# Instruction order, gate per four heads and the late weights of an attention and expert kernel

## The chip, the cores and the metric

The kernel runs on one core of one Trainium2 chip. The metric is the device time of one launch in microseconds (us), so less is better. The profile is one execution of the program, recorded by the hardware profiler.

## The reference

Windowed attention with a few global tokens is followed by a mixture of experts in which each expert keeps its 80 best tokens. There are 8 batches, 8 heads, 512 local and 32 global tokens of 64 values a head. A local query sees the local keys within 32 positions and all global keys; a global query sees every key. The 4352 token rows of 512 values then go through a gate of 8 experts.

```python
s_ll = np.where(np.abs(pos[:, None] - pos[None, :]) <= 32, scale * q_l @ k_l.T, -1e9)
a_l = sm(np.concatenate([scale * q_l @ k_g.T, s_ll], axis=-1))
out_l = a_l @ np.concatenate([v_g, v_l])
out_g = sm(scale * q_g @ np.concatenate([k_g, k_l]).T) @ np.concatenate([v_g, v_l])
x = np.concatenate([out_g, out_l], axis=2).transpose(0, 2, 1, 3).reshape(4352, 512)
logits = x @ w_gate                      # 512 x 8
expert = argmax(logits); gate_w = softmax(logits)[expert]
for e in range(8):                       # w1: 512 x 1024, w2: 1024 x 512
    tok = the 80 tokens of expert e with the largest gate_w
    out[tok] = gate_w[tok] * (relu(x[tok] @ w1[e]) @ w2[e])
```

All other rows of the output are zero.

## The kernel before

**Attention** runs in 16 steps, q = 0 to 15: a step is four heads of one batch (batch b = q // 2, quad qd = q % 2). Within a step the work is laid out by hand, and each engine runs its instructions in the order in which the program lists them. Step q computes the scores of step q + 1 and the outputs of step q:

- `load_qk` (L125) loads queries and keys as fp16 on POOL's queue, three steps ahead; `load_v` (L136) loads v on SP's queue, a batch ahead; `spread_v` (L145) copies v to `v_odd`, shifted by half a block, on POOL, and `spread_vg` (L210) the global v of four heads into the block-diagonal `vgbd`.
- `transpose_qk` (L234) transposes queries and keys on VectorE (DVE). `setup_globals` (L226) transposes the global queries and keys and spreads them into `qbd` and `kbd`, which must be cleared before.
- `S_heads` (L249) makes the local scores of two heads on TensorE (PE) and their exponentials on ScalarE (ACT). `S_globals` (L273) makes the scores with the global keys (L278), those of the global queries (L284), and the global-global ones (L279), which go into a free corner of the output tile of the running step.
- `O_pair` (L293) multiplies by v for half of the tokens, `norm` (L313) divides by the sums on DVE, `O_global` (L324) and `norm_global` (L336) do the same for the global queries.
- `x_rows` (L347) transposes the rows for the gate (L355), converts them to bf16 (ACT) and writes them to a DRAM scratch (SP). Once per batch `gate_logits` (L393), `gate_turn` (L410) and `gate_rest` (L420) compute the gate: `a0` to `a2` on DVE with one exponential, `a3` transposes the scores on PE into a list (`tp`, L462), `a4` packs row numbers and gate weights on POOL.
- `top_steps` (L486) finds the 80 best of a list in ten rounds of 8 on DVE. Three groups of batches have a list each; four rounds are done per step while there are any.

PSUM tiles come from two tags of two buffers each: S (`l_ps`, `lg`, `g_ps`, `lp`, `tp`) and O (`o_ps`). The bf16 weights of experts 0 and 1 are loaded in pieces of 256 KB during the steps (`load_w_piece`, L160).

**After attention** its pools are closed (`astack.close()`, L588), and the weights of experts 2 to 7 are issued on POOL (L593 to 596), then small constants, the clearing of `xg`, and the clearing of the rest of `pa` (L618). DVE does the last top-k, a tournament between the 64 list rows (L628, L629) that reads `pa`, the threshold and the positions; TensorE turns them into row numbers `idx`. POOL gathers the rows of the eight experts (L686), and each expert runs `F_turn` (L691), the hidden layer (L709 to 711), the output layer (L717) and the scaling by DVE into `y` (L719), a tile of three buffers:

```python
y = rpool.tile([cap, DF], FP32, tag="y", bufs=3, name=f"y{e}")
```

which POOL scatters to the output (L720). Rows that no expert takes get zeros, written by SP during the steps (`zeros`, L173).

## Time and profile before

| | us |
|---|---|
| median of 3 runs | 402.11 (400.72 to 407.21) |
| the profiled execution | 402.52 |
| its span, first to last instruction | 400.7 |
| TensorE busy | 219.0 (55%) |
| VectorE busy | 186.7 (47%) |
| POOL busy | 145.4 (36%) |
| ScalarE busy | 88.0 (22%) |

The profiled execution lies within the runs, so its rows can be used for the median. Busy shares are means over stages of different kinds; they have to be read stage by stage. L numbers are lines of the kernel before. PE is TensorE's matmuls, PEld its weight loads. The clock is the share of full speed that was granted to TensorE: 1.00 is 2.4 GHz, 0.50 is 1.2 GHz.

### The profile page before, as it was taken

The page shows a single profiled execution, that of the slowest core. Times are in us where ns is not written, and L with a number is a line of the kernel's source. Part 1 is how long each engine was busy: PE and PEld are TensorE (multiplying, and loading weights), DVE is VectorE, ACT ScalarE, POOL GpSimd, SP SyncE. Part 2 cuts the span into 40 slices and gives each one's busy share as a digit, 9 for nine tenths or more (in the row PEclk, how much of TensorE's full clock was granted, in tenths as well). Part 3 has the DMA queues.
Part 4 walks back from the last instruction along what each step waited for, and adds up shares of the span by engine and source line. Part 5 has one row for each costly group of instructions (what it writes and reads, how often), then busy time and mean ns, then how long its engine had stood idle before and what let it go on. Part 6 is the DMA issues. An engine that isn't in the chain of part 4 may idle for free. (4 is left out here: it accounts for less than half of the span.)

```text
span 400.7 us, 9267 instructions
## 1 busy us (share of the span) xinstructions
PE 219.0 (55%) x3944; PEld 154.4 (39%) x3944; DVE 186.7 (47%) x457; ACT 88.0 (22%) x153; POOL 145.4 (36%) x306
## 2 busy tenths in 40 slices
PE   1508729857857958859759759722000000347882
PEld 0306516635636736536536536511000000244561
DVE  5435665535554549667536538676700001811221
ACT  1202313325314224234324234220000000001220
POOL 8164512065074064047055053024444444052121
PEclk9966977979978786888977977955555555556999
DMA  8989247709809709907908803212999999011111
GB/s 151 177 152 240 49 79 149 201 0 181 246 16 188 224 0 181 246 2 139 277 12 159 269 0 69 97 76 70 198 209 210 209 209 207 5 41 43 34 50 33
DMA packets 60713, 51.10 MB, mean 128 GB/s; under 512 B 43904, under 2 KB 44672, under 8 KB 60672
## 3 DMA queue, kind: packets, MB, share of 16 engines
q0 software_dynamic: 19456, 27.79, 38.9%
q1 hardware_dynamic: 40112, 22.45, 21.3%
q8 instruction: 31, 0.51, 0.5%
q10 hardware_dynamic: 1104, 0.27, 0.3%
q14 instruction: 10, 0.08, 0.1%
HBM read 61.63 MB, written 14.68 MB: 190 GB/s over the span
## 5 line engine op out<-in xcount | busy, mean ns | idle before, releaser
L269 ACT ACTIVATE eL<-l_ps 128x1024 f32<-128x1024 f32 x32 | 32.8, 1024 | 98.4 <-PE l_ps L265 98.4
L473 POOL TENSOR_TENSOR rv<-oh,tb 128x160 bf16<-128x160 f32 x8 | 3.6, 456 | 136.5 <-DVE den L451 127.5
L303 PE MATMUL o_ps<-v_nat,eL 128*64 128x65 f32 x512 | 43.7, 248 | 1.3 <-issue 1.2
L303 PE MATMUL o_ps<-v_odd,eL 128*64 128x65 f32 x512 | 43.7, 249 | 0.0
L303 PEld LDWEIGHTS o_ps<-v_nat,eL 128*64 128x64 f32 x512 | 38.9, 160 | 5.2 <-issue 3.2
L308 PE MATMUL o_ps<-vgbd,eG 128*128 128x260 f32 x128 | 39.9, 437 | 0.0
L303 PEld LDWEIGHTS o_ps<-v_odd,eL 128*64 128x64 f32 x512 | 38.9, 160 | 0.0
L265 PE MATMUL l_ps<-qT,kT 32*64 32x128 f16 (+1 forms) x1152 | 26.8, 243 | 20.3 <-DVE kT L243 20.3
L642 PE MATMUL thr_ps<-dthr,ones 8*128 8x8 f32 x2 | 0.6, 352 | 66.0 <-DVE dthr L640 66.0
L265 PEld LDWEIGHTS <-kT 32*64 32x64 f16 x1152 | 20.3, 125 | 40.1 <-DVE kT L243 22.5
L711 ACT ACTIVATE fhT<-h_ps 128x320 bf16<-128x320 f32 x16 | 7.0, 437 | 111.5 <-DMA xgr<-x_scr,idx 83.7
L342 DVE RECIPROCAL rg<-o_ps 128x1 f32<-128x1 f32 x16 | 2.7, 169 | 56.4 <-PE o_ps L333 56.4
L253 PE MATMUL l_ps<-band,ident 128*128 128x512 f16 x64 | 25.4, 488 | 3.9 <-DMA band<-cband 3.9
L288 ACT ACTIVATE eG<-g_ps 128x1024 f32<-128x1024 f32 x16 | 16.4, 1024 | 46.2 <-PE g_ps L284 46.2
L642 PEld LDWEIGHTS thr_ps<-dthr,ones 8*128 8x128 f32 x2 | 0.5, 308 | 66.1 <-issue 66.1
L308 PEld LDWEIGHTS o_ps<-vgbd,eG 128*128 128x128 f32 x128 | 23.8, 207 | 4.9
L213 POOL COPY vgbd<-vg 32x65 f32<-32x65 f32 x64 | 15.2, 237 | 28.7 <-PE o_ps L333 18.7
L330 PE MATMUL o_ps<-v_nat,eG 128*32 128x65 f32 x512 | 14.5, 275 | 20.1 <-ACT egg L290 18.9
L628 DVE TENSOR_TENSOR pb<-pa 64x64 f32<-64x64 f32 x4 | 0.9, 218 | 49.7 <-POOL pa L618 49.6
L162 POOL DMA_DIRECT2D w1sb<-in_moe_w_dram x32 | 17.3, 541 | 17.0 <-DMA w1sb<-in_moe_w_dram 13.8
L320 DVE TENSOR_TENSOR xn<-o_ps,rec 128x512 f32<-128x512 f32 x32 | 22.1, 692 | 1.1
L165 POOL DMA_DIRECT2D w2sb<-in_moe_w_dram x32 | 17.2, 542 | 12.4 <-DMA w2sb<-in_moe_w_dram 12.3
(134 smaller groups left out, 479.5 us busy)
## 6 DMA issues: line engine op xcount, KB each, us to landing
out_dram<-zt SPq DMA_DIRECT2D x17, 512.0 KB, 7.2
w1sb<-in_moe_w_dram POOLq DMA_DIRECT2D x32, 256.0 KB, 9.7
w2sb<-in_moe_w_dram POOLq DMA_DIRECT2D x32, 256.0 KB, 7.1
v_nat<-in_v_l_dram SPq DMA_DIRECT2D x56, 128.0 KB, 5.7
raw<-in_q_l_dram POOLq DMA_DIRECT2D x16, 256.0 KB, 5.1
raw<-in_k_l_dram POOLq DMA_DIRECT2D x16, 256.0 KB, 7.6
x_scr<-xb SPq DMA_DIRECT2D x8, 512.0 KB, 6.5
v_nat<-in_v_l_dram SPq DMA_DIRECT2D x16, 64.0 KB, 6.3
```

Of the source, the lines that this page charges most:

```text
L162: nc.gpsimd.dma_start(out=w1sb[e][:, k], in_=moe_w1[e, 128 * k:128 * k + 128])
L165: nc.gpsimd.dma_start(out=w2sb[e][:, k].rearrange("p r f -> p (r f)"), in_=moe_w2[e, 256 * k:256 * k + 256].rearrange("(p r) f -> p (r f)" ...
L213: nc.gpsimd.tensor_copy(out=vgbd[q % 2][r, h], in_=vg[r, q])
L253: nc.tensor.matmul(out=l_ps[:, k], lhsT=ident16[:], rhs=band[:], start=True, stop=False, skip_group_check=True)
L265: nc.tensor.matmul(out=l_ps[o:o + 64, k, 64 * lo:64 * hi], lhsT=kv[r, m], rhs=qv[r, lo:hi], start=False, stop=(c2 == 1), tile_position=(32 ...
L269: nc.scalar.activation(out=eL[:], in_=l_ps[:], func=AF.Exp, scale=scale)
L288: nc.scalar.activation(out=eG[:], in_=g_ps[:], func=AF.Exp, scale=scale)
L303: nc.tensor.matmul(out=o[64 * odd:64 * odd + 64, k, 65 * h:65 * h + 65], lhsT=s["eL"][h][:, 64 * t:64 * t + 64], rhs=v[:, 4 * qd + h, u, : ...
L308: nc.tensor.matmul(out=o[:, k, 0:260], lhsT=s["eG"][:, 0, 128 * u:128 * u + 128], rhs=vgbd[q % 2][:].rearrange("p h d -> p (h d)"), start= ...
L320: nc.vector.tensor_tensor(out=s["xn"][:, 2 * j:2 * j + 2].rearrange("p u (h x) -> p u h x", x=64), in0=ov[:, :, :, 0:64], in1=rec[:].unsqu ...
L330: nc.tensor.matmul(out=og[32 * h:32 * h + 32], lhsT=s["eG"][:, 1, 128 * u + 32 * h:128 * u + 32 * h + 32], rhs=v[:, 4 * qd + h, u, :], sta ...
L711: nc.scalar.activation(out=hT[:, 4 * half:4 * half + 4, :], in_=hv, func=AF.Relu, scale=1.0)
```

## The change

The program before the steps, the order within a step, and what follows attention are laid out anew.

- **Before the steps:** `vg` is loaded in two parts, the first two quads ahead of v. Most clearing of `vg`, `vgbd`, `kbd` and `qbd` moves to DVE, for `kbd` and `qbd` only the first two quads; POOL clears the rest later. The scores of step 0 come ahead of `setup_globals`; q = 1 is transposed there too; `load_g(slice(2, 16))` moves behind the first spreads, `setup_gate` and the spread of the second half of v to the end of step 0. Constants of the routing are loaded and cleared in step 1.
- **Within a step:** `O_global` and the new `S_gg` (the global-global scores) come directly after the second `O_pair`, ahead of its norm. `x_turn` holds the transposes for the gate. `gate_logits` now does four heads at a time, those of step q - 2; `gate_turn` adds both halves. `first` holds a0 to a2; a3 and a4 come a step later, and the top-k rounds with them: three per step, five in the last two.
- **After attention:** pools are split so that the gate's tiles (`gate`, left side) outlive attention's (right side). The late weights get a pool at the right side. Two loads of 1 MB bf16 an expert take the place of eight pieces: three experts' ahead of the last `a4` and the clearing, three behind the gathers. A partition of w1 now holds four neighbouring rows instead of rows 128 apart, and `F_turn` reads the tokens with a stride to match; the pieces of w1 cover 32 partitions each.

```diff
-    astack = ExitStack()
-    apool = astack.enter_context(tc.tile_pool(name="attn", bufs=1))
-    lpool = astack.enter_context(tc.tile_pool(name="loads", bufs=2))
-    hpool = astack.enter_context(tc.tile_pool(name="heads", bufs=2))
+    gstack, astack = ExitStack(), ExitStack()
+    gpool = gstack.enter_context(tc.tile_pool(name="gate", bufs=2))
+    apool = astack.enter_context(tc.tile_pool(name="attn", bufs=1, side="right"))
+    hpool = astack.enter_context(tc.tile_pool(name="heads", bufs=2, side="right"))
...
+    def load_w1(e):
+        nc.gpsimd.dma_start(out=w1sb[e][:].rearrange("p c f -> p (c f)"),
+                            in_=moe_w1[e].rearrange("(p c) f -> p (c f)", c=4))
+
+    def load_w2(e):
+        nc.gpsimd.dma_start(out=w2sb[e][:].rearrange("p c r f -> p c (r f)"),
+                            in_=moe_w2[e].rearrange("(c p r) f -> p c (r f)", p=P, r=2))
+
     def load_w_piece(e, k):
         if k < 4:
-            nc.gpsimd.dma_start(out=w1sb[e][:, k], in_=moe_w1[e, 128 * k:128 * k + 128])
+            r = slice(32 * k, 32 * k + 32)
+            nc.gpsimd.dma_start(out=w1sb[e][r].rearrange("p c f -> p (c f)"),
+                                in_=moe_w1[e].rearrange("(p c) f -> p (c f)", c=4)[r])
...
     load_g(slice(0, 2))
     load_qk(1)
-
     ident16 = cpool.tile([P, P], FP16, name="ident16")
     nc.scalar.dma_start(out=ident16, in_=cd["ident16"].ap())
     band = apool.tile([P, 512], FP16, name="band")
     nc.scalar.dma_start(out=band, in_=cd["band"].ap().rearrange("p t i -> p (t i)"))
-
-    for i in range(2):
-        nc.vector.memset(v_nat[i][:, :, :, 64:65], 1.0)
+    identf = cpool.tile([P, P], FP32, name="identf")
+    nc.scalar.dma_start(out=identf, in_=cd["identf"].ap())
+    wgl = cpool.tile([32, 16, E], FP32, name="wgl")
+    nc.scalar.dma_start(out=wgl, in_=moe_w_gate.rearrange("(c f) e -> f c e", f=32))
+    rmask5 = cpool.tile([P, NSLOT * E], FP32, name="rmask5")
+    nc.scalar.dma_start(out=rmask5, in_=cd["rmask5"].ap().rearrange("p s e -> p (s e)"))
+    rmask = cpool.tile([P, E, NT], FP32, name="rmask")
+    nc.scalar.dma_start(out=rmask, in_=cd["rmask"].ap())
+
     kbd = apool.tile([P, NQ, 2, P], FP16, name="kbd")
     qbd = apool.tile([P, NQ, 2, P], FP16, name="qbd")
     vg = apool.tile([P, NQ, 65], FP32, name="vg")
     vgbd = [apool.tile([P, 4, 65], FP32, name=f"vgbd{i}") for i in range(2)]
     for i in range(2):
-        nc.gpsimd.memset(vgbd[i][:], 0.0)
-    nc.gpsimd.memset(vg[:, :, 64:65], 1.0)
-    nc.vector.memset(kbd[:], 0.0)
-    nc.vector.memset(qbd[:], 0.0)
+        nc.vector.memset(v_nat[i][:, :, :, 64:65], 1.0)
+    for bd in (kbd, qbd):
+        nc.vector.memset(bd[:, 0:2], 0.0)
+    nc.vector.memset(vg[:, :, 64:65], 1.0)
+    for i in range(2):
+        nc.vector.memset(vgbd[i][:], 0.0)
+    nc.sync.dma_start(out=vg[:, 0:2, 0:64], in_=v_g[0].rearrange("(q h) g d -> (h g) q d", h=4))
     load_v(0, slice(0, 4))
-    nc.sync.dma_start(out=vg[:, :, 0:64], in_=v_g.rearrange("b (q h) g d -> (h g) (b q) d", h=4))
+    nc.sync.dma_start(out=vg[:, 2:NQ, 0:64],
+                      in_=v_g.rearrange("b (q h) g d -> (h g) (b q) d", h=4)[:, 2:NQ])
+    load_v(0, slice(4, 8))
...
+    def S_gg(q, gg_ps):
+        for c2 in range(2):
+            nc.tensor.matmul(out=gg_ps, lhsT=kbd[:, q, c2], rhs=gT[:, 0, q, c2], start=False,
+                             stop=(c2 == 1), skip_group_check=True)
+
     def S_globals(q, gg_ps):
         s = st[q]
         g_ps = psS(f"g_ps{q}")
         for c2 in range(2):
             qv = qT[q][:, c2, :, 4:36].rearrange("x i (t r) -> x t i r", r=4)
             nc.tensor.matmul(out=g_ps[:, 0], lhsT=kbd[:, q, c2], rhs=qv, start=(c2 == 0), stop=(c2 == 1))
-            nc.tensor.matmul(out=gg_ps, lhsT=kbd[:, q, c2], rhs=gT[:, 0, q, c2], start=False,
-                             stop=(c2 == 1), skip_group_check=True)
...
+    def x_turn(q):
+        b, qd = divmod(q, 2)
+        bs = bst[b]
+        xT = gpool.tile([P, 8, 4, 32], FP32, tag="xT", name=f"xT{q}")
+        nc.vector.transpose(out=xT[:].rearrange("x c u i -> x u c i"),
+                            in_=st[q]["xn"][:].rearrange("p u (c x) -> p u c x", c=8))
+        xgT = gpool.tile([P, 2, 32], FP32, tag="xgT", name=f"xgT{q}")
+        nc.vector.transpose(out=xgT[:].rearrange("x c g -> x (c g)"), in_=bs["xg"][:, qd])
+        bs["xT", qd] = xT, xgT
...
+    def gate_logits(q):
+        b, qd = divmod(q, 2)
         bs = bst[b]
-        lg = psS(f"lg{b}")
-        for cc in range(16):
-            k = cc % 4
-            nc.tensor.matmul(out=lg[32 * k:32 * k + 32, 0, 0:128], lhsT=wgbd[:, cc],
-                             rhs=bs["xT"][cc // 8][:, cc % 8].rearrange("x u i -> x (u i)"),
-                             start=(cc < 4), stop=(cc >= 12), tile_position=(0, 32 * k), skip_group_check=True)
+        xT, xgT = bs["xT", qd]
+        lg = psS(f"lg{q}")
+        for j in range(8):
+            k = j % 4
+            nc.tensor.matmul(out=lg[32 * k:32 * k + 32, 0, 0:128], lhsT=wgbd[:, 8 * qd + j],
+                             rhs=xT[:, j].rearrange("x u i -> x (u i)"),
+                             start=(j < 4), stop=(j >= 4), tile_position=(0, 32 * k), skip_group_check=True)
+        for c2 in range(2):
+            nc.tensor.matmul(out=lg[0:8, 1, 0:32], lhsT=wgg[:, qd, c2], rhs=xgT[:, c2],
+                             start=(c2 == 0), stop=(c2 == 1), skip_group_check=True)
+        if qd == 0:
+            bs["lgs"] = gpool.tile([P, 2, 160], FP32, tag="lgs", name=f"lgs{b}")
+        nc.scalar.copy(out=bs["lgs"][:, qd, 0:128], in_=lg[:, 0, 0:128])
+        nc.scalar.copy(out=bs["lgs"][0:8, qd, 128:160], in_=lg[0:8, 1, 0:32])
...
+        for qd in range(2):
+            nc.tensor.transpose(out=lp[0:32, 1, 8 * qd:8 * qd + 8], in_=lgs[0:8, qd, 128:160],
+                                identity=identf[0:8, 0:8])
...
-        return [a0, a1, a2, a3, a4]
+        def first():
+            a0()
+            a1()
+            a2()
+
+        return [first, a3, a4]
...
-    setup_globals(slice(0, 2))
     transpose_qk(0, 0)
     transpose_qk(0, 1)
-    load_g(slice(2, 16))
+    S_heads(0, (0, 1))
+    S_heads(0, (2, 3))
+    setup_globals(slice(0, 2))
+    transpose_qk(1, 0)
+    transpose_qk(1, 1)
     load_qk(2)
-    nc.gpsimd.dma_start(out=tb, in_=cd["tb"].ap())
     spread_v(0, 0, 0)
     spread_v(0, 0, 1)
     spread_vg(0)
-    nc.gpsimd.memset(zt, 0.0)
-    setup_gate()
-    nc.gpsimd.memset(sc_all[:], 0.0)
-    for g in range(len(GROUPS)):
-        nc.gpsimd.memset(gp[g][:], 0.0)
-    for i in range(2):
-        nc.gpsimd.memset(Lt[i][:, 4, :], 0.0)
-    spread_v(0, 1, 0)
-    spread_v(0, 1, 1)
-    S_heads(0, (0, 1))
-    S_heads(0, (2, 3))
+    load_g(slice(2, 16))
+    for bd in (kbd, qbd):
+        nc.gpsimd.memset(bd[:, 2:], 0.0)
     gg0 = psO("gg0")
     nc.tensor.matmul(out=gg0[:, 1, 0:128], lhsT=ident16[:], rhs=ident16[:], start=True, stop=True)
+    S_gg(0, gg0[:, 1, 336:368])
     S_globals(0, gg0[:, 1, 336:368])
-    transpose_qk(1, 0)
-    transpose_qk(1, 1)
+    nc.gpsimd.memset(zt, 0.0)
 
     topq = []
-    pend = {}
+    gq = {}
     for q in range(NQ):
         b, qd = divmod(q, 2)
         nxt = q + 1 < NQ
@@ -535,6 +560,16 @@
         if qd == 0 and b + 1 < B:
             load_v(b + 1, slice(0, 8))
         zeros(1)
+        if q == 1:
+            for t, n in ((tb, "tb"), (tri, "tri"), (identbf, "identf"), (iota1, "iota1")):
+                nc.gpsimd.dma_start(out=t, in_=cd[n].ap())
+            nc.gpsimd.memset(sc_all[:], 0.0)
+            for g in range(len(GROUPS)):
+                nc.gpsimd.memset(gp[g][:], 0.0)
+            for i in range(2):
+                nc.gpsimd.memset(Lt[i][:, 4, :], 0.0)
+            nc.gpsimd.memset(onesb, 1.0)
+            nc.gpsimd.memset(ones8, 1.0)
 
         if nxt:
             S_heads(q + 1, (0, 1))
@@ -542,70 +577,78 @@
         if q + 2 < NQ:
             transpose_qk(q + 2, 0)
         norm(q, 0, o0)
-        if qd == 1 and b >= 1:
-            gate_logits(b - 1)
+        if q >= 2:
+            gate_logits(q - 2)
         if nxt:
             S_heads(q + 1, (2, 3))
         o1 = O_pair(q, 1)
+        O_global(q, o1[:, 1, 264:329])
+        if nxt:
+            S_gg(q + 1, o1[:, 1, 336:368])
         if q + 2 < NQ:
             transpose_qk(q + 2, 1)
         if q >= 1:
+            x_turn(q - 1)
+        norm(q, 1, o1)
+        norm_global(q, o1[:, 1, 264:329])
+        if nxt:
+            S_globals(q + 1, o1[:, 1, 336:368])
+        if q >= 1:
             x_rows(q - 1)
+        if qd == 0 and b >= 2:
+            gq[b - 2][1]()
         if qd == 1 and b >= 1:
             gate_turn(b - 1)
-            steps = gate_rest(b - 1)
-            for f in steps:
-                f()
+            gq[b - 1] = gate_rest(b - 1)
+            gq[b - 1][0]()
             bst.pop(b - 1)
-            for g, m in enumerate(GROUPS):
-                if m[-1] == b - 1:
-                    topq += top_steps(lst[g][:], lst[g + 1][:, 0:cap])
-        norm(q, 1, o1)
-        if nxt:
-            S_globals(q + 1, o1[:, 1, 336:368])
-        O_global(q, o1[:, 1, 264:329])
-        norm_global(q, o1[:, 1, 264:329])
+        if q == 0:
+            setup_globals(slice(2, 16))
+            setup_gate()
+            spread_v(0, 1, 0)
+            spread_v(0, 1, 1)
         if nxt:
             spread_vg(q + 1)
-        if q == 0:
-            setup_globals(slice(2, 16))
         if qd == 1 and b + 1 < B:
-            spread_v(b + 1, 0, 0)
-            spread_v(b + 1, 0, 1)
-            spread_v(b + 1, 1, 0)
-            spread_v(b + 1, 1, 1)
-        for _ in range(4):
+            for j in range(2):
+                spread_v(b + 1, j, 0)
+                spread_v(b + 1, j, 1)
+        if qd == 0 and b >= 2:
+            gq[b - 2][2]()
+            for g, m in enumerate(GROUPS):
+                if m[-1] == b - 2:
+                    topq += top_steps(lst[g][:], lst[g + 1][:, 0:cap])
+        for _ in range(5 if q >= 14 else 3):
             if topq:
                 topq.pop(0)()
+    x_turn(NQ - 1)
+    gate_logits(NQ - 2)
+    gate_logits(NQ - 1)
+    x_rows(NQ - 1)
     for f in topq:
         f()
-    x_rows(NQ - 1)
-    gate_logits(B - 1)
     gate_turn(B - 1)
-    for f in gate_rest(B - 1):
-        f()
+    gq[B - 1] = gate_rest(B - 1)
+    gq[B - 2][1]()
+    gq[B - 1][0]()
+    gq[B - 1][1]()
     zeros(17)
     astack.close()
+    wlate = ctx.enter_context(tc.tile_pool(name="wlate", bufs=1, side="right"))
+
+    def load_late(e):
+        alloc_w(e, wlate, bufs=E - NRES)
+        load_w1(e)
+        load_w2(e)
+
+    for e in range(NRES, 5):
+        load_late(e)
+    gq[B - 2][2]()
+    gq[B - 1][2]()
+    gstack.close()
...
-    w2pool = ctx.enter_context(tc.tile_pool(name="wlate", bufs=1))
-    for e in range(NRES, E):
-        alloc_w(e, w2pool, bufs=E - NRES)
-        for k in range(8):
-            load_w_piece(e, k)
-    rmask = rpool.tile([P, E, NT], FP32, name="rmask")
-    nc.sync.dma_start(out=rmask, in_=cd["rmask"].ap())
-    tri = rpool.tile([P, P], BF16, name="tri")
-    nc.gpsimd.dma_start(out=tri, in_=cd["tri"].ap())
-    identbf = rpool.tile([P, P], BF16, name="identbf")
-    nc.gpsimd.dma_start(out=identbf, in_=cd["identf"].ap())
-    iota1 = rpool.tile([P, cap], BF16, name="iota1")
-    nc.gpsimd.dma_start(out=iota1, in_=cd["iota1"].ap())
-    onesb = rpool.tile([P, P], BF16, name="onesb")
-    nc.gpsimd.memset(onesb, 1.0)
-    ones8 = rpool.tile([E, P], FP32, name="ones8")
-    nc.gpsimd.memset(ones8, 1.0)
...
+    for e in range(5, E):
+        load_late(e)
...
-            nc.tensor.transpose(out=xv[:, cc], in_=xg[e][:, 64 * cc:64 * cc + 64].bitcast(BF16),
+            nc.tensor.transpose(out=xv[:, cc], in_=xg[e][:].bitcast(BF16)[:, cc::4],
```

## Rows read from the trace of the kernel before

**Rows 1.** First line of the profile's page.
```profile
span 400.7 us, 9267 instructions
```

**Rows 2.** Stage table: start:end and length, each engine's busy us, clock, DMA share, GB/s.
```profile
0.00:61.19 61.19, 27.24 (x489) 18.03 (x489) 32.09 (x59) 11.70 (x14) 28.83 (x59) 0.83 0.84 139
61.19:253.34 192.15, 144.50 (x2864) 103.22 (x2860) 106.34 (x266) 64.88 (x111) 67.76 (x157) 0.83 0.59 138
253.34:288.90 35.56, 11.29 (x206) 8.45 (x199) 28.69 (x84) 4.42 (x12) 11.04 (x25) 0.63 0.39 87
288.90:338.54 49.64, 0.00 (x0) 0.00 (x0) 0.01 (x1) 0.00 (x0) 22.60 (x49) 0.50 1.12 209
338.54:353.23 14.69, 4.88 (x44) 3.67 (x44) 11.04 (x32) 0.00 (x0) 0.00 (x1) 0.50 0.21 32
353.23:400.70 47.47, 31.11 (x352) 21.02 (x352) 8.48 (x16) 7.00 (x16) 15.17 (x16) 0.82 0.15 42
```

**Rows 3.** Chain of waits: who waited for whom, us in total, times, longest.
```profile
DVE pb L628 <- POOL pa L618: 49.6, 1, 49.6
...
PE tp L462 <- DVE sc_all L456: 20.9, 8, 4.8
PE l_ps L265 <- DVE kT L243: 20.3, 2, 11.0
PE o_ps L279 <- DVE xn L320: 19.6, 15, 6.5
PE o_ps L330 <- ACT egg L290: 18.9, 15, 1.3
```

**Rows 4.** Order of time on POOL, 282 to 292 us: one of the paced weight issues.
```profile
286.65 0.53 POOL L162 DMA_DIRECT2D w1sb<-in_moe_w_dram  x1 [0.70 <-DMA w1sb<-in_moe_w_dram]
```

**Rows 5.** Order of time at the start, DVE, POOL, then PE: start, length, instruction, [idle before].
```profile
26.11 1.15 DVE L379 COPY wgbd<-wgl 32x128 f32<-32x128 f32 x1 [11.44 <-POOL wgbd L377]
...
44.52 1.10 DVE L228 STREAM_TRANSPOSE gT<-g 128x896 f16<-128x896 f16 x1
...
51.68 1.25 DVE L237 STREAM_TRANSPOSE qT<-raw 128x1024 f16<-128x1024 f16 x1
...
14.74 1.05 POOL L151 COPY v_odd<-v_nat 64x1040 f32<-64x1040 f32 x1 [4.40 <-DMA v_nat<-in_v_l_dram]
...
31.22 1.24 PE L265 MATMUL l_ps<-qT,kT 32*64 32x64 f16 x36 [11.05 <-DVE kT L243]
```

**Rows 6.** Order of time on PE in step q = 3 and into q = 4.
```profile
73.20 0.61 PE L253 MATMUL l_ps<-band,ident 128*128 128x512 f16 x2
...
76.48 1.08 PE L398 MATMUL lg<-xT,wgbd 128*32 128x128 f32 x32
...
77.71 0.61 PE L253 MATMUL l_ps<-band,ident 128*128 128x512 f16 x2
...
83.56 0.30 PE L462 MATMUL tp<-identf,sc_all 128*128 128x128 f32 x1 [2.27 <-DVE sc_all L456]
...
89.07 1.04 PE L253 MATMUL l_ps<-band,ident 128*128 128x512 f16 x2
```

**Rows 7.** Groups by line: the top-k rounds on DVE, total busy and mean ns.
```profile
L489 DVE MAX8 lst<-lst 128x8 f32<-128x416 f32 (+1 forms) x20 | 12.7, 633 | 0.5
...
L491 DVE MATCH_REPLACE8 lst<-lst,lst 128x416 f32<-128x416 f32 (+1 forms) x18 | 11.1, 617 | 0.0
```

**Rows 8.** Order of time near the end, DVE (the fourth y), then POOL (the last gather).
```profile
379.34 0.75 DVE L719 TENSOR_SCALAR y<-y_ps,gw 80x512 f32<-80x512 f32 x1 [1.20 <-PE y_ps L717]
...
362.19 0.96 POOL L686 DMA_INDIRECT xgr<-x_scr,idx  x1 [0.30 <-issue]
```

**Rows 9.** DMA queues and issues: packets, MB, share; KB each, median us to landing.
```profile
q0 software_dynamic: 19456, 27.79, 38.9%
...
xgr<-x_scr,idx POOLq DMA_INDIRECT x8, 2.6
...
iota<-ciota POOLq DMA_DIRECT2D x1, 20.0 KB, 6.5
```

More of the change, by code (lines that the diff above doesn't have):

```diff
@@ L126, in load_qk @@
         b, qd = divmod(q, 2)
-        raw[q] = lpool.tile([P, 2, 16, D], FP16, tag="raw", bufs=3, name=f"raw{q}")
+        raw[q] = hpool.tile([P, 2, 16, D], FP16, tag="raw", bufs=3, name=f"raw{q}")
         for t, src in ((0, q_l), (1, k_l)):
@@ L315, in norm @@
         if j == 0:
-            s["xn"] = hpool.tile([P, 4, 256], FP32, tag="xn", bufs=2, name=f"xn{q}")
+            s["xn"] = gpool.tile([P, 4, 256], FP32, tag="xn", bufs=2, name=f"xn{q}")
         ov = o[:, :, 0:260].rearrange("p u (h x) -> p u h x", x=65)
@@ L339, in norm_global @@
         if qd == 0:
-            bs["xg"] = lpool.tile([P, 2, 64], FP32, tag="xg", name=f"xg{b}")
+            bs["xg"] = gpool.tile([P, 2, 64], FP32, tag="xg", name=f"xg{b}")
         rg = hpool.tile([P, 1], FP32, tag="rg", bufs=4)
@@ L371, in x_rows @@
         st.pop(q)
-    wgbd = apool.tile([P, 16, 32], FP32, name="wgbd")
-    wgg = apool.tile([P, 2, 2, E], FP32, name="wgg")
+    wgbd = cpool.tile([P, 16, 32], FP32, name="wgbd")
+    wgg = cpool.tile([P, 2, 2, E], FP32, name="wgg")
     def setup_gate():
@@ L449, in a2 @@
             oh = t["oh"]
-            den = lpool.tile([P, NSLOT], FP32, tag="den", name=f"den{b}")
+            den = gpool.tile([P, NSLOT], FP32, tag="den", name=f"den{b}")
             nc.vector.tensor_reduce(out=den[:], in_=t["eg"][:], axis=AX.X, op=ALU.add)
-            gate = lpool.tile([P, NSLOT], FP32, tag="gate", name=f"gate{b}")
+            gate = gpool.tile([P, NSLOT], FP32, tag="gate", name=f"gate{b}")
             nc.vector.reciprocal(out=gate[:], in_=den[:])
@@ L476, in a4 @@
             src = sc_all[:, b, :, 0:E]
-            rest = lpool.tile([P, 2, NSLOT, E], FP32, tag="rest", name=f"rest{b}")
+            rest = gpool.tile([P, 2, NSLOT, E], FP32, tag="rest", name=f"rest{b}")
             for n in range(3):
```

63 lines of the change are left out of this document (22 added, 41 removed).

## Prediction

> **What bounds the kernel now.** I read the spans first, then one table of the stages, then the waits, and only then the order of time at each place. The span is 400.7 us and this execution took 402.5, so 1.8 us lie outside it; the median of the three runs is 402.1, and no scaling between them is needed [rows 1]. The stage table shows four different kernels in a row [rows 2]. From 0 to 61.2 us three of the sixteen attention steps get under way. From 61.2 to 253.3 thirteen steps run (q = 2 to 14), 14.8 us each, with TensorE busy 144.5 of 192.2 us at a mean clock of 0.83: about a third of that time is at 1.2 GHz, the rest at 2.4. From 253.3 to 288.9 the last step, its gate and the last top-k run. From 288.9 to 338.5 nothing computes: the DMA engines are full with the weights of six experts and POOL issues them. Then 14.7 us of routing, then 47.5 us from the first gather to the end.
>
> The chain of waits names three places [rows 3]. The largest is DVE waiting 49.6 us, once, for a memset of tile pa: it is 0.1 us of work, but it stands in POOL's queue behind 48 weight issues, which are paced by the DMAs ahead of them [rows 4]. In the attention steps TensorE waits 20.9 us for the gate's result (sc_all), 19.6 us because the global-key matmul L279 waits for the norm, and 18.9 us for the exponential egg, within 16 steps. Twice at the start it waits about 10 us for a transposed key tile.
>
> **The start.** Now VectorE's setup_gate sits ahead of the transposes of q = 1 and waits 11.4 us for POOL to clear wgbd [rows 5]. The change moves setup_gate to the end of step 0, loads the first eighth of vg alone, and puts vgbd's and part of kbd's and qbd's clearing on VectorE, where it is under 1 us before the first key tile lands. What is late next: the first spread of v_nat's upper half (16 us with the copies behind it, [rows 5]) and then vgbd, so that the first O_pair starts at about 18.5; before, TensorE still stood at the key tile of q = 1 until 31.2 [rows 5], ahead of the O_pair in its queue. Of that gain of 13 to 14 us not all is sure. The load of the other global keys (load_g(2:16)) goes from POOL's first issues to behind those spreads, so it leaves at 18 to 20 and, at some 12 us of transfer (my estimate: its 3,584 short packets share the DMA engines with v), lands near 32. VectorE then does setup_globals(2:16), 7.2 us from 44.5 to 51.7 in the old trace [rows 5], setup_gate (some 2 us) and the transposes and norm before the key tile of q = 3 (3.7 us). Step 2 therefore begins at about 45 instead of 61.2. The ends are 41 (the keys are there when VectorE comes) and 51 (they land at 38).
>
> **A step of attention.** I take the pieces from step 3 at the high clock [rows 6]: S_heads 1.15 us from 73.20, O_pair to 76.48, the gate's 20 matmuls to 77.71, S_heads and O_pair again to 80.9, after which comes the stall: the tp transpose waits 2.27 us, and step 4 begins only at 89.07. In the new order O_global needs nothing of this step's egg, S_gg goes ahead of the norm, the gate's half (10 matmuls, 0.6 us) uses rows turned a step before, and tp is written two steps after its logits. So the three waits go. The sum at the high clock is 1.15 + 2.15 + 0.6 + 1.15 + 2.0 + 0.7 (O_global) + 1.15 (S_globals) + 0.4 (lp or tp) = 9.3. What takes the place of the old waits: with five tiles per step in the two-buffer tag S, the next step's S_heads reuses the buffer of g_ps and must wait for eG. The nearest row for that is the egg wait of 1.26 us; lp or tp covers 0.4 of it, so I add 0.9: 10.2 us. At the low clock the band matmuls take 1.04 us instead of 0.61 [rows 6]; by that ratio a step would be 15.9. The long stalls in the old steps, such as the one at 83.56, are gone, and the low stretches came behind them; I take one step in eight low instead of a third of the time: 10.2 + 5.7 / 8 = 10.9. Bounds: 9.6 (no wait for eG, all high) and 13 (the wait stays at full size and a third stays low).
>
> VectorE does 106.3 us in those thirteen steps, 8.2 a step with the top-k in it [rows 2], so it hides behind TensorE on the mean, but not in steps 8 to 11: three top-k rounds of 0.63 + 0.62 us and what lies between, 1.35 in all [rows 7], raise it to 11 to 13. I allow 3 us for that, and 2 for v: its load and spreads take some 18 us of a pair of steps, that now lasts 22 and not 29. On POOL a4, spread_vg, spread_v and two loads a step (about 7 us) no longer stand behind a gate of the same step. The w1 pieces on 32 partitions carry the same 256 KB; I cost them at nothing: even at four times the 1.25 us of an old piece, and without that cover 5 us each, they lie inside a step. Step 15 begins at 45 + 13 x 10.9 + 5 = 192 instead of 253.3.
>
> **From step 15 to the gathers.** Before, 35.6 us pass until pa is ready but for its memset, and 14.7 more from the tournament to the first gather [rows 2]. The top-k of the second group now comes a step later, five rounds in each of steps 14 and 15 in place of four and two: of the four more rounds I count three on the path, 4.3 us with the wide list. The 49.6 us go, as only six issues stand before pa, and they carry half the weights: 24 pieces' worth at 1.25 us (0.53 of issue and 0.70 of waiting, [rows 4]) is 30 us, begun at about 10.5 us into step 15 and done at 41, beside the gate and the top-k. They need attention's buffers only, which are free by then. So the first gather leaves at 192 + 35.6 + 4.3 + 14.7 = 246.5.
>
> **From the gathers to the end.** Before, this is 47.5 us. Now the other three experts are issued right behind the eight gathers, whose last leaves 9.9 us after the first [rows 8]. All of POOL's transfers go through one queue, q0; a 20 KB table issued behind weight pieces took 6.5 us to land, against 2.6 for a gather with nothing ahead [rows 9]. So I expect the first scatter to queue behind 30 us of weights: it lands at 9.9 + 1.5 + 30 + 1 = 42.5 us after the first gather. The result tile y has three buffers, so the fourth expert's y, at 379.34 - 353.23 = 26.1 us before [rows 8], must wait for that landing. VectorE stands behind it and with it the next expert's fxT. What follows y3 now takes 400.7 - 379.3 = 21.4 us; less 1.9 (one hidden layer already done) and plus 2.5 (TensorE restarts low), the end comes 64 us after the first gather: a stall of 16.5. The strided read of xg in F_turn I put at nothing (0 to 2.5 us in all): the w1 weight loads are strided by two already and show no penalty.
>
> The Trainium skill's page "DMA: Bandwidth & Descriptors" speaks against this change: software-made DMAs have a single queue context (section "SWDGE vs HWDGE vs iDMA"), and an engine alternates between queues only (section "Queues, rings and completion order"), so a scatter could not pass the weights. By that the sum is 312, by free passage 296. The same page (section "Bandwidth") asks for transfers of 1 MiB or more and gives 6.15 us for 1 MB: by that, an estimate, six late loads would take 37 us instead of 30 and the sum would be 319. The trace moves 256 KB each 1.25 us with several in flight, so I keep 30 and expect nothing of the larger size.
>
> **The sum.** 246.5 + 64 + 1.8 = 312 us.
>
> **Rivals.**
> - The scatters do not stall (other data passes the weights, or y's wait ends early): 246.5 + 47.5 + 1.8 = 296. For it: gathers land in 2.6 us. Against: the 6.5 us of the small table.
> - The steps stay near 13 us, because the eG wait or VectorE's lag becomes the new bound and the clock keeps falling: 13 x 2.1 = 27 more, 339. For it: VectorE's mean load, and two buffers for five tiles. Against: every wait in the list has lost its cause.
> - pa stays late (the change does not do what it says): if POOL cannot put down six large loads at once and is held until they have landed at 41, the two a4 (some 2.5 us each) and the clearing of xg follow, and pa is ready at 48 instead of 40: 320.
> - Slower than before: the w1 loads in the new layout, 8 KB to a partition, run on few of the sixteen DMA engines. Three w1 loads lie ahead of the gathers with about 14 us of slack, three ahead of the scatters with none; with X us for one instead of 5 the time passes 402 when 6 (X - 5) is over 90 + 14, that is from X = 22, fewer than four engines. On one engine it would be 80 us each (5 x 16) and the kernel some 750 us. No row shows such a load; those with a row of 2 KB or more per partition do fill the engines [rows 2].
>
> **How the numbers follow.** Forecast 0.54, no stall 0.20, long steps 0.18, pa late 0.06, slow loads 0.02. The forecast's own ends, 41 to 51 for the start and 9.6 to 11.8 for a step, are 291 to 330; the first rival reaches down to 284 at a step of 10, and half of the second lies under 336. Range 284 to 336, with about 0.15 outside. A run of this kernel can tell about 2% from no change: faster by more 0.97, within 0.01, slower 0.02.
>
> **What would show it.** Right: no wait of DVE for pa; tp, L279 and egg gone from TensorE's waits and an eG wait of about 1 us per step in their place; step 2 at 41 to 51; steps near 11 us; the weights of three experts moving under the top-k; DVE's fourth y waiting 10 to 20 us on an out_dram transfer. Wrong: a step over 12 us, with DVE or ACT named ahead of S_heads; or y landing on time, which drops the stall; or a w1 load longer than 10 us.

## The result and the profile after

The changed kernel takes 308.64 us (median of 4 runs, 305.16 to 313.31) against 403.94 us for the kernel before in the same series: ratio 0.759 (95% interval 0.747 to 0.772), faster. Some executions of either kernel fall into a slower state; the ratio compares the means of the others (305.16 and 306.57 against 400.72, 402.11 and 405.78). The profiled execution took 305.2 us. L numbers from here on are lines of the changed kernel, unless it is said otherwise.

The first line of the page and the granted clock in 40 slices answer to [rows 1]:

```profile
span 303.4 us, 9280 instructions
...
PEclk9999799999999999999999998555555579655995
```

The stage table is cut at the same events as [rows 2]: start of step 2, of step 15, of the tournament, and the first gather. The stretch in which only the DMA engines worked is gone, so five lines answer to six:

```profile
0.00:42.72 42.72, 27.83 (x490) 18.75 (x490) 26.35 (x63) 9.65 (x11) 29.81 (x54) 0.96 1.08 181
42.72:178.50 135.78, 122.35 (x2897) 88.35 (x2896) 101.51 (x262) 65.59 (x122) 74.21 (x167) 1.00 0.93 196
178.50:217.94 39.44, 10.81 (x183) 7.88 (x183) 34.19 (x96) 6.64 (x21) 10.04 (x27) 0.62 0.79 176
217.94:232.62 14.68, 4.88 (x44) 3.66 (x44) 11.03 (x32) 0.00 (x0) 0.00 (x1) 0.50 0.55 106
232.62:303.40 70.78, 31.04 (x352) 20.63 (x352) 8.46 (x16) 6.99 (x16) 19.18 (x22) 0.72 0.56 117
```

The reader is to see where the 97.3 us of span went: 18.5 at the start, 56.4 in the thirteen steps, 49.6 in the pure weight stage, and in the other direction 3.9 in the last step's stage and 23.3 from the first gather to the end. In the steps TensorE's clock is 1.00 instead of 0.83; its busy time falls by 22.2 us for nearly the same matmuls (144.5 to 122.35), its idle time by 34.2 (47.6 to 13.4).

The chain of waits (columns as in [rows 3]) has lost DVE's wait for pa, the waits behind the norm and for egg, and all but 2.1 us of the 20.9 for tp. On TensorE there are small waits for eG and for VectorE's list (lst) in their place:

```profile
POOL out_dram L765 <- issue: 41.5, 6, 29.4
...
DVE y L764 <- DMA out_dram<-y,idx: 21.7, 1, 21.7
...
PE lg L421 <- DVE xgT L375: 13.7, 2, 10.1
...
PE l_ps L271 <- ACT eG L309: 5.1, 7, 0.8
...
PE l_ps L271 <- DVE lst L491: 4.7, 4, 2.9
...
PE tp L488 <- DVE sc_all L482: 2.1, 1, 2.1
```

A step's first matmul on TensorE, with the longest wait for eG that is left ([rows 6]):

```profile
63.31 0.59 PE L271 MATMUL l_ps<-band,ident 128*128 128x512 f16 x2 [0.81 <-ACT eG L309]
```

What is new on top of the chain is the scatter (L765): once POOL's issue is held for 29.4 us, and once a y waits 21.7 us for an out_dram transfer. POOL's timeline at the end (start, duration, line, what it does, in brackets the wait before it) shows both, and answers to [rows 4, 8]. First and last of the early weights, the pa clearing that was late before, the first gather, the last of the late weights, then four of the eight scatters:

```profile
190.13 0.53 POOL L161 DMA_DIRECT2D w1sb<-in_moe_w_dram  x1 [17.43 <-DVE lmax L455]
...
193.18 0.81 POOL L165 DMA_DIRECT2D w2sb<-in_moe_w_dram  x1
...
213.89 0.13 POOL L661 MEMSET pa<- 64x48 f32 x1
232.62 1.08 POOL L729 DMA_INDIRECT xgr<-x_scr,idx  x1 [18.60 <-issue]
...
245.67 0.86 POOL L165 DMA_DIRECT2D w2sb<-in_moe_w_dram  x1
246.83 0.97 POOL L765 DMA_INDIRECT out_dram<-y,idx  x1 [0.30 <-issue]
277.25 0.95 POOL L765 DMA_INDIRECT out_dram<-y,idx  x1 [29.45 <-issue]
280.68 0.91 POOL L765 DMA_INDIRECT out_dram<-y,idx  x1 [2.48 <-issue]
...
299.54 0.92 POOL L765 DMA_INDIRECT out_dram<-y,idx  x1 [4.35 <-issue]
```

The fourth and the last y on VectorE:

```profile
276.55 0.75 DVE L764 TENSOR_SCALAR y<-y_ps,gw 80x512 f32<-80x512 f32 x1 [21.74 <-DMA out_dram<-y,idx]
...
292.18 0.75 DVE L764 TENSOR_SCALAR y<-y_ps,gw 80x512 f32<-80x512 f32 x1 [2.87 <-PE y_ps L762]
```

The six early loads are put down within 4 us without being held, and pa is cleared at 214, 4 us before the tournament wants it. Behind the gathers it is otherwise. The first scatter is issued right behind the last weight, the second only 30.4 us later, 29.45 of them held, and from then on they go one at a time, 3.4 us apart: each waits 2.5 us behind the issue of the one before, about what a scatter takes to land by the table of DMA issues (count, median us to landing):

```profile
out_dram<-y,idx POOLq DMA_INDIRECT x8, 2.6
```

In the kernel before, the y's came 3.8 us apart (26.1 us to the fourth, 21.4 from there to the end, [rows 8]), so this chain hardly showed.

At the start, two rows of POOL and VectorE (they answer to [rows 5]):

```profile
25.71 3.08 POOL L541 MEMSET qbd<- 128x3584 f16 x1
...
34.46 1.47 POOL L233 COPY vgbd<-vg 32x65 f32<-32x65 f32 x4
```

```profile
28.92 1.10 DVE L246 STREAM_TRANSPOSE gT<-g 128x896 f16<-128x896 f16 x1
```

The transposition of the other global keys at 28.92 waits for nothing: their load has landed by then. The last matmuls of step 1's O_pair, which read vgbd, start at 35.98, and step 2 starts at 42.72.

### The profile page after: what moved, and what is told of

Same layout as the page of the kernel before. It is cut to its first block, busy times and chain, and to the rows that moved or that the text cites. A ratio compares the mean times of both kernels' runs of the same rounds, so it can differ in the third digit from the quotient of the medians.

```text
span 303.4 us, 9280 instructions
## 1 busy us (share of the span) xinstructions
PE 196.9 (65%) x3960; PEld 139.3 (46%) x3960; DVE 181.5 (60%) x468; ACT 88.9 (29%) x169; POOL 133.2 (44%) x269
## 3 DMA queue, kind: packets, MB, share of 16 engines
q1 hardware_dynamic: 39984, 22.29, 30.4%
## 5 line engine op out<-in xcount | busy, mean ns | idle before, releaser
L287 ACT ACTIVATE eL<-l_ps 128x1024 f32<-128x1024 f32 x32 | 32.7, 1021 | 34.2 <-PE l_ps L283 33.8
L324 PE MATMUL o_ps<-v_odd,eL 128*64 128x65 f32 x512 | 38.3, 230 | 5.4 <-POOL v_odd L151 5.4
L324 PE MATMUL o_ps<-v_nat,eL 128*64 128x65 f32 x512 | 38.6, 230 | 1.9 <-DMA v_nat<-in_v_l_dram 1.6
L762 PE MATMUL y_ps<-w2sb,fhT 128*80 128x512 bf16 x64 | 18.4, 435 | 20.0 <-DVE y L764 19.1
L271 PE MATMUL l_ps<-band,ident 128*128 128x512 f16 x64 | 20.9, 411 | 14.0 <-ACT eG L309 5.1
L340 DVE RECIPROCAL rec<-o_ps 128x8 f32<-128x8 f32 x32 | 6.4, 201 | 36.7 <-PE o_ps L293 19.5
L765 POOL DMA_INDIRECT out_dram<-y,idx x8 | 7.4, 926 | 46.5 <-issue 41.5
L764 DVE TENSOR_SCALAR y<-y_ps,gw 80x512 f32<-80x512 f32 x8 | 6.0, 747 | 33.3 <-DMA out_dram<-y,idx 21.7
L151 POOL COPY v_odd<-v_nat 64x1040 f32<-64x1040 f32 x16 | 16.8, 1050 | 16.4 <-DMA v_nat<-in_v_l_dram 9.5
L255 DVE STREAM_TRANSPOSE qT<-raw 128x1024 f16<-128x1024 f16 x16 | 19.7, 1234 | 4.4 <-DMA raw<-in_q_l_dram 4.3
L261 DVE STREAM_TRANSPOSE kT<-raw 128x512 f16<-128x512 f16 x32 | 20.7, 686 | 0.7 <-DMA raw<-in_k_l_dram 0.7
L421 PE MATMUL lg<-xT,wgbd 128*32 128x128 f32 x256 | 11.4, 297 | 14.2 <-DVE xgT L375 13.7
```

The costliest lines, as they stand in the source:

```text
L151: nc.gpsimd.tensor_copy(out=o[64:128, hs], in_=v[64:128, hs])
L255: nc.vector.transpose(out=qT[q][:, :, :, 2:34].rearrange("x c i p -> x i c p"), in_=raw[q][:, 0].rearrange("p i (c x) -> p i c x", c=2))
L261: nc.vector.transpose(out=kT[q][:, c2].rearrange("x m i r -> x i m r"), in_=raw[q][:, 1, :, 32 * c2:32 * c2 + 32])
L271: nc.tensor.matmul(out=l_ps[:, k], lhsT=ident16[:], rhs=band[:], start=True, stop=False, skip_group_check=True)
L287: nc.scalar.activation(out=eL[:], in_=l_ps[:], func=AF.Exp, scale=scale)
L324: nc.tensor.matmul(out=o[64 * odd:64 * odd + 64, k, 65 * h:65 * h + 65], lhsT=s["eL"][h][:, 64 * t:64 * t + 64], rhs=v[:, 4 * qd + h, u, : ...
```

## The experiments

The theory: the steps are short because three in-order waits are gone, and the clock stays high because of that; the stall at the end is the software queue, in which scatters stand behind weights. The main rivals: y's three buffers make the stall; the weights' place is a matter of one memset; the clock or the large loads, not the order, bring the gain. The time from the first gather to the end is read in each run's own profile, since the executions of one attention code differ (see the last section).

**More buffers for y.**

```diff
-        y = rpool.tile([cap, DF], FP32, tag="y", bufs=3, name=f"y{e}")
+        y = rpool.tile([cap, DF], FP32, tag="y", bufs=8, name=f"y{e}")
```

> The changed kernel with eight buffers for the result tile y instead of three. Theory (scatters queue behind the late weights, and each scatter is issued only when the one before has landed): DVE's wait of 21.7 us for a y buffer goes, but the first scatter still lands about 44 us after the first gather and seven more follow at 3.4 us each, so the span stays at 299 to 303 us. Rival (the three buffers alone make the stall): the span falls by the 21.7 us, to about 282.

Measured: 309.33 us, ratio 0.775 (0.769 to 0.781); from the first gather to the end 70.6 us, as with three buffers (70.8). VectorE's fourth y no longer waits, and its last one starts at 284.0 instead of 292.2, although the first gather is 4 us later in this run. POOL's scatters come no earlier:

```profile
251.21 0.98 POOL L765 DMA_INDIRECT out_dram<-y,idx  x1 [0.30 <-issue]
281.50 0.95 POOL L765 DMA_INDIRECT out_dram<-y,idx  x1 [29.31 <-issue]
...
303.80 0.92 POOL L765 DMA_INDIRECT out_dram<-y,idx  x1 [4.36 <-issue]
```

The wait of y was the sign of the stall, not its price. The end is set by the chain of scatters. With y free, TensorE meets the late weights themselves and waits twice for a w2:

```profile
PE y_ps L762 <- DMA w2sb<-in_moe_w_dram: 4.0, 2, 2.1
```

**No weights behind the gathers.** Experts 5 to 7 compute with the weights of 2 to 4; their own six loads are left out.

```diff
     for e in range(5, E):
-        load_late(e)
+        w1sb[e], w2sb[e] = w1sb[e - 3], w2sb[e - 3]
```

> The changed kernel without the loads behind the gathers: experts 5, 6 and 7 compute with the weights of experts 2, 3 and 4, so three experts' results are left out. Theory: the time from the first gather to the end falls from 70.8 to the 47.5 us of the kernel before, span about 280. Rival (the strided read of xg, the order of issues or the clock slow the expert stage, not the weights in the queue): it stays over 60 us, span over 293.

Measured: 284.33 us, ratio 0.712 (0.707 to 0.718); from the first gather to the end 45.8 us. The scatters follow the y's (first and last of eight, with the first gather):

```profile
236.27 1.07 POOL L729 DMA_INDIRECT xgr<-x_scr,idx  x1 [18.60 <-issue]
...
247.68 0.95 POOL L765 DMA_INDIRECT out_dram<-y,idx  x1 [1.48 <-DVE y L764]
...
273.98 0.91 POOL L765 DMA_INDIRECT out_dram<-y,idx  x1 [2.52 <-DVE y L764]
```

So the six loads in front of the scatters cost 70.8 less 45.8, 25.0 us; without them the tail is no longer than in the kernel before (47.5). Not all of it is the scatters' wait: the last y comes 36.7 us after the first gather here, and 47.0 after it in the run with eight buffers, where the last weights are late.

**Where the late weights stand.** Five experts' loads ahead of the gathers and one behind them, or four ahead, one behind the gathers, one behind the first scatter:

```diff
-    for e in range(NRES, 5):
+    for e in range(NRES, 7):
...
-    for e in range(5, E):
+    for e in range(7, E):
```

> The changed kernel with five experts' late weights ahead of the gathers and one behind them, instead of three and three. Theory (one queue in order, 10 us per expert): the weights begin at 190, last 50 us, so the gathers land some 7 us later than now (first at about 243); only 10 us of weights lie ahead of the first scatter, which lands before the fourth y; no stall; span about 288. Rival (transfers pass each other): gathers land as now and the span is about 280.

```diff
-    for e in range(NRES, 5):
+    for e in range(NRES, 6):
...
-    for e in range(5, E):
+    for e in range(6, 7):
...
                                      in_=y[:], in_offset=None, bounds_check=N - 1, oob_is_err=False)
+        if e == 0:
+            load_late(7)
```

> The changed kernel with four experts' late weights ahead of the gathers, one behind them, and one behind the first scatter. Theory: the four are done at about 230, just ahead of the first gather at 232.6, so the gathers are not late; the first scatter lands at about 254, the second, behind the last weights, at about 265, and six more follow at 3.4 us each: span about 287. Rival (only the buffers of y count): the fifth y waits 7 us and the span is about 287 too, but the last y then comes less than 8 us before the end.

Measured: 298.46 us (293.26 to 300.11) and 297.47 us, the latter's ratio 0.745 (0.741 to 0.750). Both are better than the change, and their spans (295.8 and 295.3) are some 8 us above what was expected. With five ahead, the first gather is at 236.9 and not, as expected, at 243, but the queue is not empty when the gathers come: the last two gathers were held by weights, and the first y came 21.8 us after the first gather instead of 11.6. In the second kernel 4.5 us of the 8 are a later first gather (237.1). There the first scatter stands behind two loads and the second behind two more; each shows as a wait of 9 to 10 us ahead of the scatter that follows:

```profile
250.16 0.97 POOL L765 DMA_INDIRECT out_dram<-y,idx  x1 [1.69 <-DVE y L764]
251.13 0.59 POOL L161 DMA_DIRECT2D w1sb<-in_moe_w_dram  x1
...
261.54 0.97 POOL L765 DMA_INDIRECT out_dram<-y,idx  x1 [9.07 <-issue]
272.50 0.95 POOL L765 DMA_INDIRECT out_dram<-y,idx  x1 [9.98 <-issue]
```

The weights in the queue are moved and only in part hidden: what stands ahead of a gather or a scatter is paid there, but from the first gather to the end it is 58.9 and 58.2 us instead of 70.8. The first kernel also shows the rate, in its ninth and tenth load of 1 MB:

```profile
202.66 0.53 POOL L161 DMA_DIRECT2D w1sb<-in_moe_w_dram  x1 [3.11 <-DMA w1sb<-in_moe_w_dram]
207.58 0.75 POOL L165 DMA_DIRECT2D w2sb<-in_moe_w_dram  x1 [4.38 <-DMA w2sb<-in_moe_w_dram]
```

**The order of the norm undone.** O_global and the global-global scores go back behind the norm.

```diff
         o1 = O_pair(q, 1)
-        O_global(q, o1[:, 1, 264:329])
-        if nxt:
-            S_gg(q + 1, o1[:, 1, 336:368])
...
         norm(q, 1, o1)
-        norm_global(q, o1[:, 1, 264:329])
         if nxt:
+            S_gg(q + 1, o1[:, 1, 336:368])
             S_globals(q + 1, o1[:, 1, 336:368])
+        O_global(q, o1[:, 1, 264:329])
+        norm_global(q, o1[:, 1, 264:329])
```

> The changed kernel with the old order behind the second O_pair: norm, then S_gg and S_globals, then O_global and its norm. Theory (TensorE is the bound of a step, so its waits add): S_gg waits for the norm by about 1.0 us and O_global for the exponential by 1.3 us again, less the wait of about 0.4 us a step for eG that they cover: some 2 us a step over 15 steps, and the clock falls at times: 30 to 40 us more before step 15 ends, span 335 to 350. Rival (VectorE or the loads are the bound of a step and hide these waits): under 8 us more, span under 315.

Measured: 353.5 us, ratio 0.884 (0.871 to 0.897), a little more than was expected. The two old waits are back, and twelve steps (2 to 13) take 163.4 us:

```profile
PE o_ps L293 <- DVE xn L341: 22.0, 15, 3.1
...
PE o_ps L351 <- ACT egg L311: 18.9, 15, 1.3
...
47.64:211.02 163.38, 130.14 (x2674) 92.11 (x2671) 96.00 (x240) 61.29 (x113) 65.93 (x150) 0.88 0.71 159
```

The same twelve steps of the change:

```profile
42.72:168.29 125.57, 112.83 (x2673) 81.48 (x2671) 96.33 (x245) 61.08 (x115) 71.69 (x160) 1.00 0.99 209
```

Of the 37.8 us between the rows, 17.3 are TensorE's busy time at a lower clock (130.14 less 112.83) and 20.5 its idle time. The idle time costs almost as much again by the clock (0.88 instead of 1.00) as by itself.

**The gate in one step.** a3 goes back behind a0 to a2 of the same odd step.

```diff
-        if qd == 0 and b >= 2:
-            gq[b - 2][1]()
...
             gq[b - 1][0]()
+            gq[b - 1][1]()
...
-    gq[B - 2][1]()
```

> The changed kernel with a3 (the transposes tp and the copies into the list) back in the odd step of its gate, directly behind a0 to a2; a4 stays a step later. Theory: in each of 7 odd steps TensorE waits for sc_all about 2.5 to 3 us, 20 us in all, and the clock falls behind some of these waits, 0 to 15 us: span 323 to 340. Rival (a step has that much slack on TensorE): less than 5 us more, span under 312.

Measured: 327.52 us, ratio 0.819 (0.808 to 0.830), as expected. Its wait and its twelve steps, 19.9 us longer at clock 0.91:

```profile
PE tp L488 <- DVE sc_all L482: 27.0, 8, 6.9
...
43.25:188.71 145.46, 124.20 (x2676) 89.13 (x2673) 99.76 (x254) 61.96 (x117) 71.82 (x162) 0.91 0.83 180
```

**Only the clearing moved, in the kernel before.** The constants and the clearing of xg and pa go ahead of the 48 weight issues.

```diff
+    pa = rpool.tile([64, P], FP32, name="pa")
+    pb = rpool.tile([64, P], FP32, name="pb")
+    nc.gpsimd.memset(pa[:, cap:P], 2.0)
     w2pool = ctx.enter_context(tc.tile_pool(name="wlate", bufs=1))
     for e in range(NRES, E):
...
```

> The kernel before with one edit: the small constants, the clearing of xg and that of pa stand ahead of the 48 weight issues instead of behind them. Theory (the 49.6 us are the time of the weights, which stay ahead of the gathers in POOL's queue and in the transfer queue): routing runs at 289 to 304 beside the weights, but the first gather leaves only when POOL is done with its issues, at about 333, and lands near 343 instead of 356; span 385 to 390. Rival (the memset alone holds the kernel up): the full 49.6 us go, span about 352.

Measured: 392.78 us, ratio 0.982 (0.971 to 0.994); its span, 391.2, is just above the 385 to 390 that were expected. The pa wait is gone and the gathers take its place behind the weights (lines of the kernel before, moved by a few):

```profile
PE xT_ps L696 <- DMA xgr<-x_scr,idx: 43.8, 1, 43.8
```

So the 49.6 us were not the memset's; they were the queue's, and moving the memset alone does not take them away.

**Small pieces for the early weights.** Three experts as 24 pieces of 256 KB instead of six loads of 1 MB; the six loads behind the gathers stay whole.

```diff
-        load_w1(e)
-        load_w2(e)
+        for k in range(8):
+            load_w_piece(e, k)
...
     for e in range(NRES, 5):
...
```

> The changed kernel with the three experts' weights ahead of the gathers issued in eight pieces of 256 KB each (w1 pieces on 32 partitions) instead of two loads of 1 MB. Theory (the queue moves 256 KB in 1.25 us whatever the size of a transfer, and POOL is held after some eight issues, but is done before pa is needed): 24 pieces end about 30 us after the first, pa is cleared before the last top-k ends, span as now, 303 to 309. Rival 1 (large transfers are the faster ones): the pieces take 38 us and more and the gathers come late by some us. Rival 2 (pieces on 32 partitions use fewer engines): a w1 piece takes 2.5 us or more, the weights end near 236 and the gathers land 4 us or more late, span over 308.

Measured: 314.33 us, ratio 0.783 (0.771 to 0.796). The expected span, "as now", was wrong. Nine pieces go down at once; from the tenth on each waits for an earlier one, and POOL is held until 219, so the last a4 comes late and VectorE waits 4.7 us for it and 1.6 us more for pa. The tenth and the last piece, POOL's next work, and that wait from the chain of waits:

```profile
197.14 0.50 POOL L171 DMA_DIRECT2D w1sb<-in_moe_w_dram  x1 [0.87 <-DMA w1sb<-in_moe_w_dram]
...
218.57 0.53 POOL L175 DMA_DIRECT2D w2sb<-in_moe_w_dram  x1 [0.71 <-DMA w2sb<-in_moe_w_dram]
219.12 0.47 POOL L499 TENSOR_TENSOR rv<-oh,tb 128x160 bf16<-128x160 f32 x1
...
DVE hi L663 <- POOL rv L505: 4.7, 1, 4.7
```

From the start of step 14 to the first gather it is 70.8 us instead of 64.3 (64.3 or 64.4 in four more runs of the same code). The large loads are worth 6.4 us, by freeing POOL: the two waits of VectorE are all of it.

**The start.** The rest of kbd and qbd is cleared by VectorE.

```diff
     for bd in (kbd, qbd):
-        nc.gpsimd.memset(bd[:, 2:], 0.0)
+        nc.vector.memset(bd[:, 2:], 0.0)
```

> The changed kernel with the rest of kbd and qbd cleared on DVE, idle at that time, and not on POOL. Theory (POOL's queue, with two clearings of 3.1 us ahead of the spread of v's second half, sets the start of step 1's O_pair, and not the landing of the global keys): that O_pair's last matmuls end some 6 us earlier, at about 32 instead of 37.9; step 2 is then bound by setup_globals on DVE and begins at 40 to 41 instead of 42.7; the total falls by about 2 us, too little to tell. Rival (the keys' load sets it): nothing moves at the start.

Measured: 309.51 us, ratio 0.771 (0.761 to 0.782). The last matmuls of step 1's O_pair end at 34.2 instead of 37.9, 3.7 us earlier and not 6; VectorE clears each tile in 1.55 us, POOL took 3.1. Step 2 starts at 40.32 instead of 42.72, where six other runs with the old start have 42.0 to 43.3:

```profile
40.32 0.59 PE L271 MATMUL l_ps<-band,ident 128*128 128x512 f16 x2
```

Step 3 starts about where it did (52.92 against 52.56), and nothing is left at the end.

**Two versions that go further.** In the first, the w1 of a third expert is loaded during the steps too (raw gets two buffers and rmask is loaded after attention, for room), eight loads of 1 MB stand ahead of the gathers, one behind them, one behind each of the first two scatters. The second also regroups the lists, so that no step has more than three top-k rounds:

```diff
-GROUPS = [[0, 1, 2], [3, 4, 5], [6, 7]]
+GROUPS = [[0, 1, 2], [3, 4], [5, 6, 7]]
...
-        for _ in range(5 if q >= 14 else 3):
+        for _ in range(3):
```

> The changed kernel with fewer weights behind the gathers: w1 of expert 2 is loaded during the steps as well (two raw buffers instead of three and rmask loaded after attention make room); eight loads of 1 MB stand ahead of the gathers, w2 of expert 6 behind them, w1 of expert 7 behind the first scatter and w2 of expert 7 behind the second. Theory: the 40 us of weights end before the first gather, no scatter has more than 5 us of weights ahead of it, no y waits, and the time from the first gather to the end is 46 to 49 us as without these loads; span 279 to 286. Rival (each scatter still waits for the one before, and the weights between them add up): 54 us, span 287 to 293.

> The version of the last batch with the top-k groups cut as batches 0-2, 3-4 and 5-7 instead of 0-2, 3-5 and 6-7, three rounds a step throughout. Theory (the ten rounds of the second group in steps 14 and 15 delay VectorE by some 7 us before the last gate, and the last list grows by 128 columns, 10 rounds x 0.25 us): the time from the start of step 15 to the first gather falls from about 54 to 49 us, steps 12 to 14 take 2 us more; span 3 us less than without, about 284. Rival (the rounds only move, VectorE is as late in step 15): no difference.

Measured: 287.88 us, ratio 0.715 (0.705 to 0.725), with 51.5 us from the first gather to the end, between the theory and its rival; its span, 287.2, is the rival's. The first gather and the first four scatters:

```profile
235.72 1.07 POOL L737 DMA_INDIRECT xgr<-x_scr,idx  x1 [19.72 <-issue]
...
250.65 0.97 POOL L772 DMA_INDIRECT out_dram<-y,idx  x1 [4.12 <-DVE y L771]
...
255.62 0.95 POOL L772 DMA_INDIRECT out_dram<-y,idx  x1 [3.40 <-issue]
...
261.24 0.95 POOL L772 DMA_INDIRECT out_dram<-y,idx  x1 [3.88 <-DMA out_dram<-y,idx]
267.69 0.92 POOL L772 DMA_INDIRECT out_dram<-y,idx  x1 [5.50 <-DVE fxT L750]
```

Beside the weights the scatters go 5.0, 5.6 and 6.5 us apart instead of 3.4. With the new groups 281.98 us, ratio 0.700 (0.689 to 0.710), the best kernel of the study: from the start of step 14 to the first gather it takes 56.4 us instead of 64.3, more than was expected. Its first gather:

```profile
226.78 1.07 POOL L737 DMA_INDIRECT xgr<-x_scr,idx  x1 [19.36 <-issue]
```

## Why the prediction was right, and where it was not

**The start** was put at 45 and is 42.7; that the number is close is luck, as the reason is not the one named. The other global keys were to land near 32 and be what is late; the trace has them transposed at 28.92 without a wait. What is late is POOL: its two clearings of 3.1 us each stand ahead of the second spread and of vgbd. The run with the clearing on VectorE shows it: 2.4 us come back at step 2. What still holds that O_pair for 2.4 us then, its trace does not name.

**The steps** were put at 10.9 us and 5 us more in all, 147 us; they are 10.4 us, 135.8 in all. That the order is what counts is shown by the two runs that undo a part of it (47 and 21.5 us more of span). The wait for eG is there as foreseen, at most 0.8 us against 0.9, but only 7 times; 4 times VectorE's list is late instead. The term that was mis-sized is the clock: one step in eight was put low, and none is, which is 9.3 us of the 10.9. The allowance for the top-k rounds (3 us) was right: twelve steps take 9.8 to 10.9 us, and step 10 takes 12.1, with a wait of 2.9 for VectorE's list. That for v (2 us) was not needed.

**From step 15 to the gathers** 54.6 us were foreseen and 54.1 measured. The early weights run beside the gate and the top-k. But the working took the size of a load to be worth nothing, and the run with pieces shows that 6.4 us hang on it: the rival in which POOL is held (8 us) did not come about because six large loads go down at once. The top-k rounds do cost: with four of them in steps 14 and 15 instead of ten, the way from step 14 to the gathers is 8 us shorter, 1.3 us a round. By that the four more rounds are some 5 us, an estimate, against the 4.3 that were put.

**From the gathers to the end** 64 us were foreseen and 70.8 measured. The mechanism is shown from both sides: without the loads 45.8, with more y buffers 70.6. The way to the fourth y was put at 42.5 and is 43.9; that y waits 21.7 us, a little over the 10 to 20 named as a sign. The step that failed is what follows it: "What follows y3 now takes 21.4" was carried over with small corrections to 22 us, and 26.9 were measured, because behind the stall the end is set by the scatters, not by the experts. That scatters go one at a time stands in no term of the sum: the second leaves at 277.25, beside that fourth y, and the other six follow at 3.4 us and, for the last, 5.3.

The Trainium skill's page "DMA: Bandwidth & Descriptors" (section "SWDGE vs HWDGE vs iDMA") allots software-made DMAs one queue, and the trace agrees that a scatter does not pass the loads ahead of it: POOL is held for 29.45 us here. The Trainium skill's 6.15 us for 1 MB on the same page (section "Bandwidth") is more than this case shows for loads in a row: in the run with five experts ahead, POOL is held by the loads in flight, and the two held issues of 1 MB are 4.92 us apart (202.66 and 207.58), near the 30 us of the prediction for six.

The sum was 310.3 of span against 303.4: the steps 11 us better, the start 2 better, the tail 7 worse. That it came so close is in part luck, since the errors of the steps and of the tail have opposite signs. Of the rivals, the one without a stall had the right tail for a kernel without loads there (47.5, measured 45.8); the one with long steps is what the two kernels with an undone order became.

## What to carry to other kernels

Ask of each transfer what stands ahead of it in its own queue: bulk loads in one software queue with gathers and scatters are paid by whichever small transfer comes next. Moving them within the queue gave back only half of the bill here (12 of 25 us from the first gather to the end); 19 came back with one w1 more loaded during the steps and the rest spread further. In an engine's fixed order, put what depends on nothing new ahead of what waits for another engine; the two waits that came back added 1.7 us of idle time to each step here and 3.2 us to its length, because TensorE's clock fell with them. When a stall is taken over from an old trace, look also at the chain behind it, which may have been hidden only because the work above it was slower.
